# First chunk of a fused attention and two-FFN kernel: a weight piece's head and low part one tick behind its sign, and every second piece's join and low part on VectorE

## The chip, the cores and the metric

One core of a Trainium2 chip runs the whole program. The metric is device microseconds of one execution. TensorE (PE in the profile) multiplies, VectorE (DVE), ScalarE (ACT) and GpSimd (POOL) do the element-wise work, and SyncE (SP) issues the transfers. Each engine takes its instructions in the order in which they were written, and waits for others by semaphores.

## The reference, cut to what matters

```python
x = attention(q, k, v)             # 4 batches, 8 heads, 576 x 64; half the heads local, half strided
h = x @ w_in                       # 2304 x 512 @ 512 x 2048
x = (h - np.tanh(h)) @ w_out       # 2048 x 512
g, val = x @ w_gate, x @ w_val     # 512 x 1536 each
return (g / (1 + np.exp(-g)) * val) @ w_out2
```

Everything is float32 (the host reads pairs of float32 weights as int64). The change touches how `w_in` and `w_out` are made ready, and one small step of the attention's softmax.

## The kernel before, in words

The 2304 tokens are worked through in five chunks of 512 (one of 256). For each chunk the first FFN runs over 16 column blocks, f = 0 to 15: twelve matmuls of 128x512 give `ps_h` (`first_part`), `bend` takes tanh on ScalarE (L520) and subtracts on VectorE (L521), `parts` splits the result into a high and a low half on ScalarE (L527) and VectorE (L528), and twelve matmuls add the block to `ps_acc` (`second`, one iteration later). Every product is taken as three matmuls, high by low, high by high and low by high (L191 to L193), so every weight must exist as a high half and a low half.

During the first chunk two more streams share the engines. One is the attention of the second batch, in twelve groups: its scores (PE, L265), mask and row maximum (VectorE, three times L273), exp (ScalarE, L282), the reciprocal of the row sum (ScalarE L290 adds 1e-9, VectorE L294), the multiplication by it (GpSimd, L296), transposes (PE, L308), the copy of them (VectorE, L312) and the product with v (PE, L320). The other is the feed: the weights arrive as 32 pieces of 128x512 int64 words, each of them read as a low int32 word and a high one, and every piece goes through

- `high` and `low` on ScalarE (L124, L127),
- `rebase` on VectorE: `clamp` (L130) and `shift` (L134),
- `join` on GpSimd: an int32 addition (L142),
- `sign` on VectorE (L146),
- `head` on ScalarE, which rounds to the high half (L152), and `rest` on GpSimd, which subtracts it for the low half (L155).

Pieces 0 to 3 (`PRE`) are made during the attention of the first batch. From then on `Feed.tick` is called twice in an iteration: once after `bend` and the product with v, and once after `second` and exp. Tick t starts the load of piece t + 2, takes piece t through `high` and `low`, piece t - 1 through `rebase` and `join`, and piece t - 2 through `sign`, `head` and `rest`. Iteration f multiplies with pieces 2f - 1 and 2f, and its ticks are 4 + 2f and 5 + 2f. The order on each engine is the order in which the code is written; no scheduler moves it in this part of the program.

Of the kernel before, what the change touches and what calls it, by code (L numbers as in the profile page):

```python
# [7 lines left out]
F32 = mybir.dt.float32  # L8
# [5 lines left out]
AF = mybir.ActivationFunctionType  # L14
ALU = mybir.AluOpType
# [18 lines left out]
BV = 2  # L34
# [21 lines left out]
STREAMED = (3, 7, 11, 15)  # L56
# [5 lines left out]
PRE = 4  # L62
# [11 lines left out]
def model_kernel(ctx: ExitStack, tc: tile.TileContext, q, k, v, mask, ident, sq, sk, sv, smask, w1, w2, out):  # L74
    nc = tc.nc
# [34 lines left out]
        return mpool.tile([P, 512], F32, tag=mtags[-1], name="m")  # L110

    class Piece:
        def __init__(self, key, src, place, then=None):
            self.key, self.src, self.place, self.then = key, src, place, then

        def load(self):
            self.st = stage.tile([P, 512], I64, tag="st", name="st")
# [21 lines left out]

        def join(self):  # L140
            mi = self.m.bitcast(I32)
            nc.gpsimd.tensor_tensor(out=mi, in0=mi, in1=self.lo, op=ALU.add)  # L142

        def sign(self):
            mi = self.m.bitcast(I32)
# [6 lines left out]
            nc.scalar.copy(self.w[:, 0, :], self.m)  # L152

        def rest(self):
            nc.gpsimd.tensor_tensor(out=self.w[:, 1, :], in0=self.m, in1=self.w[:, 0, :].bitcast(F32), op=ALU.subtract)  # L155
            if self.then:
                self.then(self.w)

    class Feed:
# [18 lines left out]
        def tick(self):  # L178
            t = self.at
            self.at += 1  # L180
            self.load(t + 3)
            self.do(t, "high", "low")
            if t - 1 >= self.since:
                self.do(t - 1, "rebase", "join")
            if t - 2 >= self.since:
                self.do(t - 2, "sign", "head", "rest")

    def mm3(ps, w, c0, xh, xl, start, stop, goes_on=False):

# [5 lines left out]
    with tc.manual_schedule():  # L195
# [56 lines left out]
        class Group:  # L252
# [25 lines left out]
            def exp(self):  # L278
                w = self.w
                self.sm = att.tile([P, 16], F32, tag="sm", name="sm", bufs=3)[:, :GB]  # L280
                for i in range(GB):
                    nc.scalar.activation(  # L282
                        self.s[:, i, :w], self.s[:, i, :w], AF.Exp, scale=-1.0, bias=self.mx[:, i:i + 1],
                        **({"accum_out": self.sm[:, i:i + 1]} if self.b else {}),
                    )

            def norm(self, eng):
                w = self.w
                if self.b:
                    nc.scalar.activation(self.sm, self.sm, AF.Copy, bias=1e-9)  # L290
                else:
                    nc.vector.tensor_reduce(out=self.sm, in_=self.s[:, :, :w], axis=AX, op=ALU.add)
                    nc.vector.tensor_scalar(self.sm, self.sm, 1e-9, None, ALU.add)
                nc.vector.reciprocal(self.sm, self.sm)  # L294
                if eng is nc.gpsimd:
                    nc.gpsimd.tensor_tensor(  # L296
                        out=self.s[:, :, :w], in0=self.s[:, :, :w], in1=self.sm.unsqueeze(2).to_broadcast([P, GB, w]),
                        op=ALU.mult,
                    )
                    return  # L300
                for i in range(GB):
                    s, r = self.s[:, i, :w], self.sm[:, i:i + 1]
                    nc.scalar.mul(s, s, r)
# [142 lines left out]
        w1_t, w2_t = {}, {}  # L446
        resident = [f for f in range(NF1) if f not in STREAMED]
        uses = sorted((f + part, part, f) for f in range(NF1) for part in range(2))
# [3 lines left out]
        def slot_of(f, part, c=0):  # L452
            if f in STREAMED:
                return 2 * NRES + (c * NS + stream.index((f, part))) % NSS
            return 2 * resident.index(f) + part

        def piece1(f, part):
            def spill(w):
                nc.sync.dma_start(out=w1s[stream.index((f, part))], in_=w.bitcast(F32))

            return Piece((f, part), w1[f, :, part * 512:(part + 1) * 512], lambda: wtile(f"w{slot_of(f, part)}"),
                         spill if f in STREAMED else None)

        def wtile(tag):
            return wpool.tile([P, 2, 512], F32R, tag=tag, name=tag)
# [13 lines left out]
        def restore():  # L479
            while fetching:  # L480
                c, i = fetching.pop(0)
                w = w1_t[stream[i]] = wtile(f"w{slot_of(*stream[i], c)}")
                nc.sync.dma_start(out=w.bitcast(F32), in_=w1s[i])

        feed1 = Feed([piece1(f, part) for _, part, f in uses], w1_t)

        def halves(xh, xl, src, dh, dl):
            nc.scalar.copy(dh, src)
# [29 lines left out]
        def bend(ps, n):  # L518
            t = epool.tile([P, CHUNK], F32, tag="e", name="t")
            nc.scalar.activation(t[:, :n], ps[:, :n], AF.Tanh)  # L520
            nc.vector.tensor_tensor(out=ps[:, :n], in0=ps[:, :n], in1=t[:, :n], op=ALU.subtract)  # L521
            return ps
# [54 lines left out]
        ahead, late, order = [], [], PAIRS  # L577
# [168 lines left out]
        class Quad:  # L746
# [54 lines left out]
            def prepare(self):  # L801
# [23 lines left out]
                for s in range(2):  # L825
# [27 lines left out]
                    s4 = flow.add("G", 0.78, lambda pool=pool: pool("d", right, "b", right, "m", right, ALU.subtract, "bm"), (s2, s3))  # L853
                    h1 = flow.add("A", 0.4, half, (a, *((h1,) if s else ())), None if s else slots)
                    self.ends[s, 4] = flow.add("V", 0.45, rest, (h1,))
                    later.append((s2, s4))
                for i, (name, src, products) in enumerate((("w2", "m", (5, 6)), ("w3", "d", (7, 3)))):
# [157 lines left out]
        for c, (c0, n) in enumerate(CHUNKS1):  # L1015
# [10 lines left out]
            for f in range(NF1):  # L1026
# [26 lines left out]
                t = bend(ps, n)  # L1053
# [91 lines left out]
        late = ctx.enter_context(tc.tile_pool(name="late", bufs=1, side="right", reuse_waits="tile"))  # L1145
# [158 lines left out]
        for t in range(2):  # L1304
# [18 lines left out]
            for p in ORDER3:  # L1323
                flow.until(lambda: len(G[t, p]) == NQ and all(left(p, q)[0] is not None for q in range(NQ)),
                           [*W3[{1: 0, 2: 1, 4: 1, 5: 2, 6: 2}.get(p, 3)], *G3[t, p]])
                for m in range(2):
                    place = {1: "a", 6: "a", 5: "a", 3: "a", 2: "b", 7: "c", 4: "c"}[p]
# [131 lines left out]
```

## Time and profile before

| | us |
|---|---|
| median of 3 runs (lowest, highest) | 923.49 (920.88, 923.81) |
| the profiled execution | 920.19 |
| its span | 918.3 |
| PE busy in the span | 880.8 (96%) |
| VectorE, ScalarE, GpSimd busy | 644.5, 458.7, 337.5 |
| first chunk, from the tanh of f = 2 to that of f = 12 | 78.91 (58.30 to 137.21) |
| from there to the second chunk's first tanh | 30.53 |

PE's busy time is nearly the span, so the kernel is bound by PE wherever PE finds its inputs ready. The page's picture in 40 slices of 23 us shows PE at 8 tenths in the first three slices and in the seventh and eighth (138 to 184 us), and at 9 in nearly all others. TensorE's granted clock is at full level (2.4 GHz) from the third slice on. To read how an iteration of the first chunk goes, one takes the engines' rows of one iteration in order of time and sees which row begins late, and which lasts longer than others of its kind. A row's duration includes the time for which the instruction was held up after it had begun.

### The profile page before, as it was taken

The page shows a single profiled execution, that of the slowest core. Times are in us where ns is not written, and L with a number is a line of the kernel's source. Part 1 is how long each engine was busy: PE and PEld are TensorE (multiplying, and loading weights), DVE is VectorE, ACT ScalarE, POOL GpSimd, SP SyncE. Part 2 cuts the span into 40 slices and gives each one's busy share as a digit, 9 for nine tenths or more (in the row PEclk, how much of TensorE's full clock was granted, in tenths as well). Part 3 has the DMA queues.
Part 4 walks back from the last instruction along what each step waited for, and adds up shares of the span by engine and source line. Part 5 has one row for each costly group of instructions (what it writes and reads, how often), then busy time and mean ns, then how long its engine had stood idle before and what let it go on. Part 6 is the DMA issues. An engine that isn't in the chain of part 4 may idle for free. (4 is left out here: it accounts for less than half of the span.)

```text
span 918.3 us, 14160 instructions
## 1 busy us (share of the span) xinstructions
PE 880.8 (96%) x4918; PEld 722.3 (79%) x4918; DVE 644.5 (70%) x1222; ACT 458.7 (50%) x1034; POOL 337.5 (37%) x284
## 2 busy tenths in 40 slices
PE   8889998899999999999999988999999999999998
PEld 6567776777877778998887776888888887888888
DVE  6778786677776787326886785788877777966451
ACT  5577775534244523225555454555545446655431
POOL 2578887385526553001503421535544320000000
PEclk9899999999999999999999999999999999999999
DMA  8464743632343210426636642535452568968551
GB/s 272 154 195 155 255 158 113 241 110 82 103 140 118 69 46 24 146 85 237 221 92 205 207 149 82 183 117 165 154 184 87 200 216 291 344 229 278 198 202 42
DMA packets 66215, 150.38 MB, mean 164 GB/s; under 512 B 7200, under 2 KB 13344, under 8 KB 66144
## 3 DMA queue, kind: packets, MB, share of 16 engines
q1 hardware_dynamic: 65568, 149.04, 48.3%
q8 instruction: 39, 0.64, 0.3%
q10 hardware_dynamic: 576, 0.43, 0.2%
q14 instruction: 32, 0.26, 0.1%
HBM read 105.93 MB, written 43.52 MB: 163 GB/s over the span
## 5 line engine op out<-in xcount | busy, mean ns | idle before, releaser
L193 PE MATMUL ps_acc<-sl 128*128 128x512 f32 (+1 forms) x336 | 126.7, 377 | 5.0 <-DVE sl L738 5.0
L191 PE MATMUL ps_acc<-sl 128*128 128x512 f32 (+1 forms) x336 | 126.8, 377 | 3.4 <-ACT t L1206 3.4
L191 PE MATMUL ps_acc<-gl,w 128*128 128x512 f32 (+1 forms) x320 | 123.2, 385 | 3.4 <-DVE gl L528 3.3
L192 PE MATMUL ps_acc<-sl 128*128 128x512 f32 (+1 forms) x336 | 126.4, 376 | 0.0
L191 PE MATMUL ps_h<-xl,w 128*128 128x512 f32 (+1 forms) x320 | 121.1, 379 | 1.9 <-DVE gl L528 1.9
L193 PE MATMUL ps_h<-xh,w 128*128 128x512 f32 (+1 forms) x320 | 118.5, 370 | 0.7 <-POOL w L155 0.7
L193 PE MATMUL ps_acc<-gh,w 128*128 128x512 f32 (+1 forms) x320 | 118.5, 370 | 0.0
L192 PE MATMUL ps_acc<-gh,w 128*128 128x512 f32 (+1 forms) x320 | 118.3, 370 | 0.0
L192 PE MATMUL ps_h<-xh,w 128*128 128x512 f32 (+1 forms) x320 | 118.1, 369 | 0.0
L142 POOL TENSOR_TENSOR sl<-sl,st 128x512 int32<-128x512 int32 x36 | 52.0, 1450 | 164.6 <-DVE sl L134 134.2
L520 ACT ACTIVATE t<-ps_h 128x512 f32<-128x512 f32 (+1 forms) x80 | 44.0, 550 | 110.9 <-PE ps_h L193 110.9
L521 DVE TENSOR_TENSOR ps_h<-ps_h,t 128x512 f32<-128x512 f32 (+1 forms) x80 | 51.5, 643 | 65.5 <-ACT t L520 65.1
L976 DVE TENSOR_TENSOR sl<-sl 128x512 fp32r<-128x512 f32 (+1 forms) x120 | 73.9, 669 | 28.5 <-ACT sl L972 27.8
L528 DVE TENSOR_TENSOR gl<-ps_h,gh 128x512 fp32r<-128x512 f32 (+1 forms) x80 | 51.1, 638 | 39.5 <-ACT gh L527 38.0
L972 ACT CAST sl<-sl 128x512 fp32r<-128x512 f32 (+1 forms) x120 | 65.7, 599 | 25.2 <-DMA sl<-gd 19.0
L193 PEld LDWEIGHTS ps_acc<-sl 128*128 128x128 f32 x336 | 63.7, 190 | 17.2 <-DVE sl L738 5.9
L191 PEld LDWEIGHTS ps_acc<-sl 128*128 128x128 f32 x336 | 63.7, 190 | 16.8 <-ACT t L1206 5.5
L191 PEld LDWEIGHTS ps_acc<-gl,w 128*128 128x128 f32 x320 | 60.3, 188 | 18.5 <-DVE gl L528 6.0
L386 POOL TENSOR_TENSOR pr<-skv,sq 128x576 f32<-128x576 f32 (+8 forms) x40 | 56.3, 1437 | 50.2 <-DVE sc L393 30.6
L191 PE MATMUL ps_a<-sl 128*128 128x512 f32 (+1 forms) x192 | 70.3, 366 | 2.7 <-DVE t L1167 2.7
L192 PEld LDWEIGHTS ps_acc<-sl 128*128 128x128 f32 x336 | 63.6, 189 | 11.2
L193 PEld LDWEIGHTS ps_h<-xh,w 128*128 128x128 f32 x320 | 60.5, 189 | 11.8 <-POOL w L155 1.5
(125 smaller groups left out, 1960.9 us busy)
## 6 DMA issues: line engine op xcount, KB each, us to landing
st<-in_w SPq DMA_DIRECT2D x68, 512.0 KB, 4.7
gd<-t SPq DMA_DIRECT2D x84, 256.0 KB, 2.1
sl<-gd SPq DMA_DIRECT2D x84, 256.0 KB, 4.5
w<-w1s SPq DMA_DIRECT2D x32, 512.0 KB, 3.5
w3s<-sl SPq DMA_DIRECT2D x24, 256.0 KB, 4.0
sl<-w3s SPq DMA_DIRECT2D x24, 256.0 KB, 5.4
x2d<-o SPq DMA_DIRECT2D x18, 256.0 KB, 3.2
out_t<-t SPq DMA_DIRECT2D x18, 256.0 KB, 2.1
```

Source lines behind the costliest of these rows:

```text
L142: nc.gpsimd.tensor_tensor(out=mi, in0=mi, in1=self.lo, op=ALU.add)
L191: nc.tensor.matmul(ps, lhsT=wh, rhs=xl, start=start, stop=False, skip_group_check=goes_on)
L192: nc.tensor.matmul(ps, lhsT=wh, rhs=xh, start=False, stop=False, skip_group_check=goes_on)
L193: nc.tensor.matmul(ps, lhsT=wl, rhs=xh, start=False, stop=stop, skip_group_check=goes_on)
L386: nc.gpsimd.tensor_tensor(out=t, in0=x, in1=y, op=ALU.mult)
L520: nc.scalar.activation(t[:, :n], ps[:, :n], AF.Tanh)
L521: nc.vector.tensor_tensor(out=ps[:, :n], in0=ps[:, :n], in1=t[:, :n], op=ALU.subtract)
L528: nc.vector.tensor_tensor(out=gl[:, :n], in0=t[:, :n], in1=gh[:, :n].bitcast(F32), op=ALU.subtract)
L972: nc.scalar.copy(got[0][:, 0, :n], got[0][:, 1, :n].bitcast(F32))
L976: nc.vector.tensor_tensor(out=w[:, 1, :n], in0=w[:, 1, :n].bitcast(F32), in1=w[:, 0, :n].bitcast(F32), op=ALU.subtract)
```

## The change

Three things change.

1. In `tick`, piece t - 3 now gets `head` (it was t - 2, together with its sign). `rest` of that piece follows at once in odd ticks, and stands at the end of the tick in even ones. `sign` of piece t - 2 comes before `high`, `low`, `rebase` and `join` of the later pieces.
2. Pieces from 4 on with an odd number get `join` and `rest` on VectorE; the others stay on GpSimd. That is fourteen pieces, 5 to 31.
3. In the second batch's attention the addition of 1e-9 stands directly behind exp, and no longer at the start of the next iteration.

```diff
         def join(self):
             mi = self.m.bitcast(I32)
-            nc.gpsimd.tensor_tensor(out=mi, in0=mi, in1=self.lo, op=ALU.add)
+            self.eng.tensor_tensor(out=mi, in0=mi, in1=self.lo, op=ALU.add)
...
         def rest(self):
-            nc.gpsimd.tensor_tensor(out=self.w[:, 1, :], in0=self.m, in1=self.w[:, 0, :].bitcast(F32), op=ALU.subtract)
+            self.eng.tensor_tensor(out=self.w[:, 1, :], in0=self.m, in1=self.w[:, 0, :].bitcast(F32), op=ALU.subtract)
...
             self.load(t + 3)
-            self.do(t, "high", "low")
-            if t - 1 >= self.since:
-                self.do(t - 1, "rebase", "join")
-            if t - 2 >= self.since:
-                self.do(t - 2, "sign", "head", "rest")
+            late = t % 2 == 0
+            for back, *steps in (
+                (3, "head", *(() if late else ("rest",))), (2, "sign"), (0, "high", "low"), (1, "rebase", "join"),
+                (3, *(("rest",) if late else ())),
+            ):
+                if t - back >= self.since:
+                    self.do(t - back, *steps)
...
+                if 0 < self.b < BV:
+                    nc.scalar.activation(self.sm, self.sm, AF.Copy, bias=1e-9)
...
-                if self.b:
+                if self.b >= BV:
                     nc.scalar.activation(self.sm, self.sm, AF.Copy, bias=1e-9)
-                else:
+                if not self.b:
...
-        def piece1(f, part):
+        def piece1(i, f, part):
...
-                         spill if f in STREAMED else None)
+                         spill if f in STREAMED else None, nc.vector if i >= PRE and i % 2 else nc.gpsimd)
```

VectorE's order in the middle of the first chunk, before, from the copy of one group's transposes (L312) to the last feed step ahead of the next group's mask and maximum; `m` is the piece being made, `ps_h` and `gl` belong to the FFN:

```order
L312 COPY pt<-ps_a 80x384
L528 TENSOR_TENSOR gl<-ps_h,gh 128x512
L130 TENSOR_SCALAR m<-m 128x512
L134 TENSOR_SCALAR m<-m 128x512
L146 SCALAR_TENSOR_TENSOR m<-st,m 128x512
L294 RECIPROCAL sm<-sm 128x3
L521 TENSOR_TENSOR ps_h<-ps_h,t 128x512
L130 TENSOR_SCALAR m<-m 128x512
L134 TENSOR_SCALAR m<-m 128x512
L146 SCALAR_TENSOR_TENSOR m<-st,m 128x512
```

The same stretch now (lines are up to four higher: L316 is L312, L532 is L528, L298 is L294, L525 is L521):

```order
L316 COPY pt<-ps_a 80x384
L532 TENSOR_TENSOR gl<-ps_h,gh 128x512
L146 SCALAR_TENSOR_TENSOR m<-st,m 128x512
L130 TENSOR_SCALAR m<-m 128x512
L134 TENSOR_SCALAR m<-m 128x512
L298 RECIPROCAL sm<-sm 128x3
L525 TENSOR_TENSOR ps_h<-ps_h,t 128x512
L146 SCALAR_TENSOR_TENSOR m<-st,m 128x512
L130 TENSOR_SCALAR m<-m 128x512
L134 TENSOR_SCALAR m<-m 128x512
L142 ISA m<-st,m 128x1024
L155 TENSOR_TENSOR w_1220<-m,w_1220 128x512
```

The two signs (L146) have moved ahead of the clamp and shift of their tick, and the odd pieces' join and rest stand at the end. The join has become a custom instruction on 1024 halves of words (`ISA`), since VectorE takes 512 int32 words so.

GpSimd's order over two iterations, before; `s` is a group's softmax, `w` a finished weight:

```order
L155 TENSOR_TENSOR w_1007<-m,w_1007 128x512
L296 TENSOR_TENSOR s<-s,sm 128x3x80
L142 TENSOR_TENSOR m<-m,st 128x512
L155 TENSOR_TENSOR w_1046<-m,w_1046 128x512
L142 TENSOR_TENSOR m<-m,st 128x512
L155 TENSOR_TENSOR w_1096<-m,w_1096 128x512
L296 TENSOR_TENSOR s<-s,sm 128x3x80
L142 TENSOR_TENSOR m<-m,st 128x512
L155 TENSOR_TENSOR w_1135<-m,w_1135 128x512
L142 TENSOR_TENSOR m<-m,st 128x512
```

And now (L300 is L296):

```order
L155 TENSOR_TENSOR w_1087<-m,w_1087 128x512
L142 TENSOR_TENSOR m<-m,st 128x512
L300 TENSOR_TENSOR s<-s,sm 128x3x80
L155 TENSOR_TENSOR w_1176<-m,w_1176 128x512
L142 TENSOR_TENSOR m<-m,st 128x512
L300 TENSOR_TENSOR s<-s,sm 128x3x80
L155 TENSOR_TENSOR w_1272<-m,w_1272 128x512
L142 TENSOR_TENSOR m<-m,st 128x512
L300 TENSOR_TENSOR s<-s,sm 128x288
```

An iteration had two joins, two rests and a multiplication on GpSimd, and has one of each now; the join stands directly ahead of the multiplication, and the rest ahead of the join.

## Rows read from the trace of the kernel before

**Rows 1.** Busy time by engine, two stretches: us, then each engine's.

```profile
core 0: us, PE busy (x) PEld busy (x) DVE busy (x) ACT busy (x) POOL busy (x), PEclk, DMA share, GB/s
58.30:137.21 78.91, 72.71 (x498) 54.73 (x497) 64.56 (x161) 58.44 (x161) 65.67 (x51) 1.00 0.60 194
137.21:167.74 30.53, 26.63 (x131) 19.71 (x130) 21.11 (x35) 17.44 (x37) 18.60 (x15) 1.00 0.34 120
```

**Rows 2.** Waits from 50 to 165 us: in total, times, longest.

```profile
ACT w L152 <- DVE m L146: 29.9, 26, 2.4
...
PE ps_a L308 <- POOL s L296: 7.4, 11, 1.5
```

**Rows 3.** VectorE in order of time, one iteration: start us, us.

```profile
84.47 0.68 DVE L146 SCALAR_TENSOR_TENSOR m<-st,m 128x512 int32<-128x512 int32 x1
85.07 0.23 DVE L273 CUSTOM_DVE_ANT_0 s<-ps_a,mask_s 128x80 f32<-128x80 f32 x1
...
85.55 0.54 DVE L312 COPY pt<-ps_a 80x384 f32<-80x384 f32 x1
86.32 0.69 DVE L528 TENSOR_TENSOR gl<-ps_h,gh 128x512 fp32r<-128x512 f32 x1 [0.22 <-ACT gh L527]
86.93 0.94 DVE L130 TENSOR_SCALAR m<-m 128x512 f32<-128x512 f32 x1
87.90 0.43 DVE L134 TENSOR_SCALAR m<-m 128x512 int32<-128x512 int32 x1
...
90.21 0.70 DVE L521 TENSOR_TENSOR ps_h<-ps_h,t 128x512 f32<-128x512 f32 x1 [0.31 <-ACT t L520]
90.81 0.82 DVE L130 TENSOR_SCALAR m<-m 128x512 f32<-128x512 f32 x1
```

**Rows 4.** GpSimd in order of time, the same iteration.

```profile
86.28 1.30 POOL L155 TENSOR_TENSOR w<-m,w 128x512 fp32r<-128x512 f32 x1
88.46 1.63 POOL L142 TENSOR_TENSOR m<-m,st 128x512 int32<-128x512 int32 x1 [0.88 <-POOL w L155]
90.05 1.31 POOL L155 TENSOR_TENSOR w<-m,w 128x512 fp32r<-128x512 f32 x1
91.31 0.77 POOL L296 TENSOR_TENSOR s<-s,sm 128x240 f32<-128x240 f32 x1
```

**Rows 5.** VectorE's clamp and shift with GpSimd idle, around 50 us.

```profile
49.66 0.42 DVE L130 TENSOR_SCALAR m<-m 128x512 f32<-128x512 f32 x1
...
50.11 0.43 DVE L134 TENSOR_SCALAR m<-m 128x512 int32<-128x512 int32 x1
```

**Rows 6.** GpSimd's join and multiplication around 51 us.

```profile
50.67 1.31 POOL L142 TENSOR_TENSOR m<-m,st 128x512 int32<-128x512 int32 x1 [2.39 <-ACT s L282]
51.94 0.59 POOL L296 TENSOR_TENSOR s<-s,sm 128x240 f32<-128x240 f32 x1
```

**Rows 7.** Lines L738 and L890 in the whole run: ns minimum, median, maximum.

```profile
L738 DVE TENSOR_TENSOR sl<-sl x67: 677/684/1800, 426.4 to 734.3; 128x512 fp32r<-128x512 f32 x67
L890 DVE TENSOR_TENSOR sl<-sl x8: 1211/1219/2225, 458.1 to 540.0; 128x1024 f32<-128x1024 f32 x8
```

**Rows 8.** ScalarE in order of time: first exp, high, head of an iteration.

```profile
86.18 0.36 ACT L282 ACTIVATE s<-s,mx 128x80 f32<-128x80 f32 x1
...
87.23 0.67 ACT L124 ACTIVATE m<-st 128x512 f32<-128x512 f32 x1
...
88.96 0.62 ACT L152 CAST w<-m 128x512 fp32r<-128x512 f32 x1 [0.48 <-DVE m L146]
```

**Rows 9.** ScalarE's tanh of f = 2, of f = 12, of the second chunk's f = 0.

```profile
58.30 0.58 ACT L520 ACTIVATE t<-ps_h 128x512 f32<-128x512 f32 x1
...
137.21 0.58 ACT L520 ACTIVATE t<-ps_h 128x512 f32<-128x512 f32 x1
...
167.74 0.60 ACT L520 ACTIVATE t<-ps_h 128x512 f32<-128x512 f32 x1 [2.08 <-PE ps_h L193]
```

More of the change, by code (lines that the diff above doesn't have):

```diff
@@ L112, in model_kernel, with __init__ @@
     class Piece:
-        def __init__(self, key, src, place, then=None):
-            self.key, self.src, self.place, self.then = key, src, place, then
+        def __init__(self, key, src, place, then=None, eng=nc.gpsimd):
+            self.key, self.src, self.place, self.then, self.eng = key, src, place, then, eng
         def load(self):
@@ L483, in restore @@
                 nc.sync.dma_start(out=w.bitcast(F32), in_=w1s[i])
-        feed1 = Feed([piece1(f, part) for _, part, f in uses], w1_t)
+        feed1 = Feed([piece1(i, f, part) for i, (_, part, f) in enumerate(uses)], w1_t)
         def halves(xh, xl, src, dh, dl):
```

## The prediction

> **What bounds the kernel now.** I read the busy time by stretches first. From the tanh of f = 2 to that of f = 12 of the first chunk, ten full iterations, PE is busy for 72.71 of 78.91 us [rows 1, 9]: an iteration takes 7.89 us, and PE idles for 0.62 of it. In the rest of the chunk it is busy for 26.63 of 30.53 us [rows 1]. So at most 6.2 + 3.9 = 10.1 us are to be had where the change works, and later chunks gain or lose only by starting earlier or later.
>
> Then the waits. PE waits 11 times, 7.4 us in all, for GpSimd's softmax multiplication before a transpose, and ScalarE spends 29.9 us with its head waiting for VectorE's sign [rows 2]. Both are what the change goes at.
>
> Third, the two timelines side by side, for who makes GpSimd late. The reader is to compare rows of one kind. VectorE's clamp takes 0.42 us and its shift 0.43 when GpSimd is idle [rows 5]. In the iteration the clamp at 86.93 takes 0.94, and ends at 87.87: 0.42 behind 87.45, while GpSimd's rest ends at 87.58 [rows 3, 4]. The clamp at 90.81 takes 0.82 and ends 0.42 behind 91.21, with GpSimd's rest ending at 91.36. Both were held until about 0.13 to 0.15 us before the end of GpSimd's record. The other way round, GpSimd's join takes 1.31 us undisturbed [rows 6] but 1.63 at 88.46 [rows 4], when it starts while a sign runs. So VectorE's clamp, shift and sign and all of GpSimd's instructions hold each other off; one at a time gets through, and the one that waits comes next. Instructions of VectorE that read PSUM are not held: the mask (0.23) and L521 (0.70) have their usual lengths beside GpSimd's work [rows 3]. The stage is therefore bound by this alternation between VectorE and GpSimd, with 65.67 us of GpSimd and 64.56 of VectorE in 78.91 [rows 1], and PE's waits are its result.
>
> **The change part by part.** It takes from GpSimd, in an iteration, one join and one rest: 1.31 + 1.30 = 2.61 us [rows 4, 6]. That leaves under 4 of its 6.6 us, so GpSimd is no longer short of time. It gives VectorE these two.
>
> The rest on VectorE is a float32 subtraction of two SBUF operands, 128x512: 0.684 us median [rows 7]. The join is not in the trace. It handles 512 words, as 1024 halves. By the sign, which reads the same strided words, it would be 0.68 [rows 3]; by L890 with its 1024 elements, 1.22 [rows 7]. I take 0.78, since the bytes are the sign's, and keep 0.68 and 1.22 for the range. Below 0.68 there is nothing: no two-operand row of 512 words is shorter. The Trainium skill, VectorE: DVE Perf Modes, "What auto-detection actually checks", has two-source instructions on 16-bit operands of step 1 run at double rate; by that the 1024 halves would take no longer than 512 words, and the sum would be about 1 us lower. No row here shows such an instruction.
>
> Head behind its sign by a tick: the 29.9 us of ScalarE's waiting go, since a sign is a tick old when its head comes. That frees tanh, which stood behind the head, and I count 0.5 us for it in the first two iterations. ScalarE is not the bound afterwards. The 1e-9 addition, moved behind exp, is done before the reciprocal comes to its turn; the reciprocal is hidden below, so I count nothing for it.
>
> What is late next is VectorE. I lay one iteration of it out in the new order, from the end of an even piece's shift to the next such end. Back-to-back instructions start about 0.08 us before the record of the one ahead ends (85.07 against 84.47 + 0.68) [rows 3], so the pitches below are shorter than durations.
> - GpSimd's join starts 0.13 behind the shift (88.33 to 88.46) [rows 3, 4] and takes 1.31 [rows 6]. The next sign needs just this join: 1.44. The reciprocal and L521 (0.70) are hidden in it.
> - GpSimd's multiplication stands right behind the join and gets in ahead of the sign: 0.59 less 0.13 for the 80-wide groups, more for the 96-wide: 0.50 [rows 6].
> - Sign 0.60 (84.47 to 85.07), clamp 0.45, shift 0.43 [rows 3, 5].
> - Join 0.70 and rest 0.60, as pitches.
> - Mask and maximum 0.48 (85.07 to 85.55), copy 0.46, L528 0.61 (86.32 to 86.93), sign 0.60, clamp 0.45 [rows 3, 5].
> - Shift 0.43, held by GpSimd's rest. This rest comes when ScalarE has done three exps (86.18 to 87.23, 1.05 us) and a head (0.62) [rows 8], begun with the mask: some 1.8 to 2.1 us behind it, which is just when clamp and shift are due (0.48 + 0.46 + 0.61 + 0.60 = 2.15). Of its 1.30 less 0.13 I count 0.95 as VectorE's loss; between 0 and 1.17 is possible.
>
> The sum is 1.44 + 0.50 + 1.48 + 1.30 + 2.60 + 1.38 = 8.70 us, against 7.89: 0.81 more. PE (7.27 busy) and ScalarE (5.84) [rows 1] lie beside it. Ten iterations lose 8.1 us. The rest of the chunk comes to 8.2 for an iteration without the mask and three of 8.70 - 0.50 - 0.48 - 0.46 = 7.3 without any softmax, 30.1 against 30.5: about even. With 0.5 us won at the start, that is 7.6 to 8.1; I take 8.
>
> A weight comes a tick later now. It is still made in the iteration before the one that uses it, some 8 us ahead, so I cost that at nothing; with VectorE behind by more than an iteration it would appear as PE waiting for a rest. The loads come from a five-buffer pool whose buffers are freed by signs, which come earlier in the tick; nothing there. The loss is carried to the end, for the later chunks are ordered behind the first on PE.
>
> By the profiled execution, 920.19 + 8 = 928.2; that run is 3.3 under the median of those shown, so against the median 923.5 + 8 = 931.5.
>
> **The rivals.**
>
> *GpSimd's relief wins.* If the two stalls of VectorE, 0.50 and 0.95, don't arise, because the rest falls beside the copy and L528, which read PSUM, and the multiplication behind the sign, an iteration is 8.70 - 1.45 = 7.25, and PE's 7.27 decides. Then all of PE's idle time goes: 923.5 - 10.1 = 913.4. For it speaks that GpSimd has half its time free. Against it: the rest cannot start before exp and head, which wait for the mask, and these put it on the clamp, not on the copy. The Trainium skill, GPSIMD Engine Reference, "4.1 Engine selection", puts element-wise additions on VectorE, as about twice as fast there. That is true of each instruction here (0.68 against 1.30 for a rest), and by it alone this rival would be the forecast.
>
> *One stall stays.* With the rest hidden and the multiplication not, or the other way round, an iteration is 7.75 to 8.2: between -1.4 and +3 us, around 923.
>
> *The join at 1.22.* As the forecast, with 0.44 more in each of some thirteen iterations: +5.7, so 937.
>
> *The change does not do what it says:* if VectorE still waited for GpSimd's pieces, its sign would; it does, for the even ones, and that is in the sum.
>
> **How the numbers follow.** The forecast 0.57, the slow join 0.15, one stall 0.14, relief 0.14. The two slower cases lie above 926.3 but for a tail of 0.02. Of the middle case 0.06 is faster by over 0.3% (under 920.7), 0.05 within, 0.03 slower; 0.3%, 2.8 us, is about what can be told from no change. So faster 0.20, same 0.07, slower 0.73. The forecast's own range is 927 to 935. Eight tenths need most of the slow join and the middle case: 919 to 938.
>
> **What would show it.** In the changed profile tanh starts of neighbouring iterations would be 8.5 to 8.9 us apart. VectorE would be busy for more than 90% of the ten iterations and GpSimd for some 40%. The odd ticks' clamp or shift would last 1.2 us or more beside a rest of GpSimd's, and the sign of an even piece would wait for GpSimd's join or last longer than 1 us. ScalarE's head would no longer wait for a sign. It is wrong if iterations are 7.9 us or less, if shift and clamp keep their 0.43, or if the join takes less than 0.6 or over 1.3.

## The result, and the profile after

The changed kernel takes 933.42 us (median of 4 runs, 931.52 to 934.88), the kernel before 922.74 in the runs beside it (4 runs, 920.88 to 923.81): a ratio of 1.0117, 95% interval 1.0091 to 1.0143. Slower, as forecast, 1.9 us above the forecast and inside its own range.

Busy time by stretches in the profile after, in the columns of [rows 1]: the ten iterations, then the rest of the first chunk.

```profile
61.81:147.87 86.06, 74.00 (x505) 55.08 (x500) 77.07 (x180) 58.12 (x161) 33.59 (x31) 1.00 0.59 178
147.87:180.21 32.34, 27.97 (x136) 20.95 (x137) 25.85 (x43) 18.21 (x38) 9.62 (x9) 1.00 0.32 112
```

An iteration takes 8.61 us (7.89 before), and the rest of the chunk 1.81 us more than 30.53. VectorE is busy for 77.07 of 86.06 us (90%), and GpSimd's share has fallen from 83% to 39%. The profiled execution takes 934.88 us, 14.7 more than before. Of these, 3.95 arise ahead of the first tanh (50.78 against 46.83), where nothing was changed; a second profile of the same kernel (below) has it at 48.25, so they are not put down to the change. 8.5 arise from there to the second chunk's first tanh, and 2.2 behind that. These last are not put down to the change either: 2.8 are lost between 570 and 600 us, where the granted clock is 0.89 in this execution and 1.00 in the same stretch, counted from the second chunk's first tanh, of the second profile and of the kernel before; the remainder of the run wins some of it back.

VectorE in order of time, one iteration after, against [rows 3]. L525 was L521, L298 L294, L275 L273, L316 L312 and L532 L528; the number in brackets is the engine's idle time just before the row, and what ended it. The dots behind the first shift stand for the reciprocal (0.16 us).

```profile
86.03 0.42 DVE L130 TENSOR_SCALAR m<-m 128x512 f32<-128x512 f32 x1
86.48 1.40 DVE L134 TENSOR_SCALAR m<-m 128x512 int32<-128x512 int32 x1
...
87.88 0.67 DVE L525 TENSOR_TENSOR ps_h<-ps_h,t 128x512 f32<-128x512 f32 x1
89.36 1.06 DVE L146 SCALAR_TENSOR_TENSOR m<-st,m 128x512 int32<-128x512 int32 x1 [0.81 <-POOL m L142]
90.34 0.41 DVE L130 TENSOR_SCALAR m<-m 128x512 f32<-128x512 f32 x1
90.79 0.43 DVE L134 TENSOR_SCALAR m<-m 128x512 int32<-128x512 int32 x1
91.25 0.69 DVE L142 CUSTOM_DVE_ANT_0 m<-st,m 128x1024 uint16<-128x1024 uint16 x1
91.86 0.68 DVE L155 TENSOR_TENSOR w<-m,w 128x512 fp32r<-128x512 f32 x1
92.46 0.23 DVE L275 CUSTOM_DVE_ANT_0 s<-ps_a,mask_s 128x80 f32<-128x80 f32 x1
...
92.94 0.55 DVE L316 COPY pt<-ps_a 80x384 f32<-80x384 f32 x1
93.42 0.68 DVE L532 TENSOR_TENSOR gl<-ps_h,gh 128x512 fp32r<-128x512 f32 x1
94.01 0.68 DVE L146 SCALAR_TENSOR_TENSOR m<-st,m 128x512 int32<-128x512 int32 x1
94.61 0.42 DVE L130 TENSOR_SCALAR m<-m 128x512 f32<-128x512 f32 x1
95.06 1.39 DVE L134 TENSOR_SCALAR m<-m 128x512 int32<-128x512 int32 x1
```

GpSimd beside it, against [rows 4, 6]:

```profile
86.13 1.46 POOL L155 TENSOR_TENSOR w<-m,w 128x512 fp32r<-128x512 f32 x1 [4.84 <-DVE m L146]
88.01 1.32 POOL L142 TENSOR_TENSOR m<-m,st 128x512 int32<-128x512 int32 x1 [0.42 <-DVE sm L298]
89.28 0.59 POOL L300 TENSOR_TENSOR s<-s,sm 128x240 f32<-128x240 f32 x1
```

Read the two together. The shift at 86.48 ends at 87.88, 0.43 behind 87.45; GpSimd's rest ends at 87.59. So the shift was held until 0.14 before the end of that record. GpSimd's join begins 0.13 behind the shift's end, and the sign at 89.36 begins 0.03 behind the join's end. That sign then lasts 1.06 instead of 0.68: GpSimd's multiplication, in order right behind the join, got in ahead of it. These are the two stalls that the forecast named, and the 0.81 is VectorE's only idle time in the iteration.

The waits of the same stretch (50 to 175 us), against [rows 2]:

```profile
POOL w L155 <- DVE m L146: 48.7, 10, 4.9
...
PE ps_h L195 <- DVE w L155: 16.4, 13, 2.7
DVE m L146 <- POOL m L142: 9.3, 11, 1.1
...
ACT w L152 <- DVE m L146: 2.7, 2, 2.2
```

ScalarE's head waits for 2.7 us in all (29.9 before). GpSimd now waits for VectorE, and PE for the rest that VectorE makes, not for the softmax.

### The profile page after: what moved, and what is told of

It reads as the page before. It is cut to its first block, busy times and chain, and to the rows that moved or that the text cites. A ratio compares the mean times of both kernels' runs of the same rounds, so it can differ in the third digit from the quotient of the medians.

```text
span 933.0 us, 14169 instructions
## 1 busy us (share of the span) xinstructions
PE 887.5 (95%) x4918; PEld 727.0 (78%) x4918; DVE 661.5 (71%) x1250; ACT 459.8 (49%) x1034; POOL 293.7 (31%) x256
## 5 line engine op out<-in xcount | busy, mean ns | idle before, releaser
L195 PE MATMUL ps_h<-xh,w 128*128 128x512 f32 (+1 forms) x320 | 120.8, 378 | 16.4 <-DVE w L155 16.4
L194 PE MATMUL ps_h<-xh,w 128*128 128x512 f32 (+1 forms) x320 | 119.6, 374 | 0.0
L525 DVE TENSOR_TENSOR ps_h<-ps_h,t 128x512 f32<-128x512 f32 (+1 forms) x80 | 51.2, 640 | 65.7 <-ACT t L524 65.3
L532 DVE TENSOR_TENSOR gl<-ps_h,gh 128x512 fp32r<-128x512 f32 (+1 forms) x80 | 50.9, 636 | 32.5 <-ACT gh L531 31.0
```

The source lines that it names most:

```text
L194: nc.tensor.matmul(ps, lhsT=wh, rhs=xh, start=False, stop=False, skip_group_check=goes_on)
L195: nc.tensor.matmul(ps, lhsT=wl, rhs=xh, start=False, stop=stop, skip_group_check=goes_on)
L532: nc.vector.tensor_tensor(out=gl[:, :n], in0=t[:, :n], in1=gh[:, :n].bitcast(F32), op=ALU.subtract)
```

## The experiments

Two explanations stand against each other. The first is the forecast's: the new order puts GpSimd's join right ahead of a sign that needs it, its multiplication ahead of that sign too, and its rest on a clamp or shift. The second: VectorE has more work, two instructions more in an iteration, wherever they stand. Each kernel was profiled and timed beside the kernel before. Diffs are against the changed kernel.

**The order alone.** The new order, every join and rest on GpSimd.

```diff
-                         spill if f in STREAMED else None, nc.vector if i >= PRE and i % 2 else nc.gpsimd)
+                         spill if f in STREAMED else None, nc.gpsimd)
```

> The new order of the ticks alone; every join and rest stays on GpSimd. Theory A (the order): a sign now stands directly behind its GpSimd join, so VectorE waits out the join in both ticks, and GpSimd's rest still holds a clamp or shift; iterations of 8.5 to 8.8 us and a time of 929 to 935 us, as slow as the whole change without VectorE doing any more work. Theory B (the added work): what costs is the join and rest that VectorE took on, 1.37 us an iteration; without them an iteration is 7.9 us or less, and the time 915 to 924 us.

Measured: 934.17 us, ratio 1.0129 (1.0105 to 1.0153). With VectorE relieved of all that the change gave it, the loss is as large. The iteration takes 8.79 on average, or 8.53 without the first one, which takes 11.13 (PE waits there for a rest of GpSimd's, 3.1 us). It is another iteration, though: VectorE waits for a tanh, and its clamp is held by two rests of GpSimd's that follow each other. VectorE, then GpSimd:

```profile
85.01 1.51 DVE L130 TENSOR_SCALAR m<-m 128x512 f32<-128x512 f32 x1
...
87.83 0.70 DVE L525 TENSOR_TENSOR ps_h<-ps_h,t 128x512 f32<-128x512 f32 x1 [0.75 <-ACT t L524]
```

```profile
83.27 2.97 POOL L155 TENSOR_TENSOR w<-m,w 128x512 fp32r<-128x512 f32 x2
```

So the order by itself is enough for the loss, but this run does not show that it is by the same two stalls.

**The move alone.** The old order, odd pieces on VectorE.

```diff
-            late = t % 2 == 0
-            for back, *steps in (
-                (3, "head", *(() if late else ("rest",))), (2, "sign"), (0, "high", "low"), (1, "rebase", "join"),
-                (3, *(("rest",) if late else ())),
...
+            self.do(t, "high", "low")
+            if t - 1 >= self.since:
+                self.do(t - 1, "rebase", "join")
+            if t - 2 >= self.since:
+                self.do(t - 2, "sign", "head", "rest")
```

> The old order of the ticks; the odd pieces' join and rest on VectorE. Theory A (the order): a whole tick lies between a join and its sign, so VectorE waits for no join; its added work replaces time in which GpSimd held it; iterations of 7.9 to 8.2 us, a time of 921 to 927 us. Theory B (the added work): VectorE's 1.37 us more per iteration come on top, iterations of 8.5 us or more, 930 us or more.

Measured: 925.43 us, ratio 1.0034 (1.0016 to 1.0052), 8.08 an iteration. The move costs about 3 us in the old order and nothing measurable in the new one (933.42 with it, 934.17 without). The trace shows a new wait and a hold: the rest now stands on VectorE in the tick of its sign and head, and waits for the head there. How much of the 3 us they carry was not tried.

```profile
85.46 1.00 DVE L155 TENSOR_TENSOR w<-m,w 128x512 fp32r<-128x512 f32 x1 [0.73 <-ACT w L152]
```

**GpSimd's rest made small.** The even pieces' rest on 16 columns; the remaining columns of their low half are filled by ScalarE with other data, so those weights are not the reference's.

```diff
-            self.eng.tensor_tensor(out=self.w[:, 1, :], ...
+            n = 16 if self.small else 512
+            self.eng.tensor_tensor(out=self.w[:, 1, :n], ...
...
```

> The changed kernel with the even pieces' rest on GpSimd cut to 16 of 512 columns (the rest of the low half is filled with other numbers by ScalarE, in its idle time ahead of exp, so the output is not the reference's). Theory A, as in the prediction's sum: the shift loses its hold of 0.95 us and nothing else is near, so iterations fall from 8.61 to about 7.7 us and the time by 9 to 11 us, to 922 to 925. Theory A2: tanh is next, since in the changed kernel it ends only 0.2 us ahead of VectorE's L525; iterations stay at 8.3 to 8.5 us and the time falls by 2 to 3 us.

Measured: 918.28 us, ratio 0.995 (0.9931 to 0.9968), 7.67 an iteration. That is 0.94 less than 8.61, and the shift's row shows where it went (L532 is here the subtraction behind tanh, L525 above):

```profile
89.98 0.43 DVE L134 TENSOR_SCALAR m<-m 128x512 int32<-128x512 int32 x1
...
91.21 0.70 DVE L532 TENSOR_TENSOR ps_h<-ps_h,t 128x512 f32<-128x512 f32 x1 [0.72 <-ACT t L531]
```

1.40 less 0.43 is 0.97. One hold of one instruction so carries the whole of the loss and some more. It also shows VectorE's chain as the pace: what was taken from it came out of the iteration nearly one to one. Theory A2 priced tanh as the next limit. VectorE does wait for tanh now, 0.72 us, but in the time in which it would wait for GpSimd's join anyway, so this costs nothing. The time is under theory A's 922 to 925; the rest of the chunk, which it left out, is 3.0 us shorter too (29.30 against 32.34).

**The multiplication made small.** GpSimd's multiplication of the first chunk on 4 columns of each group; the other softmax weights stay unnormalised.

```diff
+                    w = 4 if self.b == 1 else w
                     nc.gpsimd.tensor_tensor(
```

> The changed kernel with GpSimd's softmax multiplication of the first chunk's groups cut to 4 columns (the rest of the weights stays unnormalised, so part of the computation is left out). In the changed kernel's trace the multiplication takes 0.59 us, starts right behind GpSimd's join and ahead of VectorE's sign, and the sign then takes 1.06 instead of 0.69 us. If VectorE's chain sets the pace, the sign comes back to about 0.69 and an iteration falls from 8.61 by 0.37 to 0.5 us, to 8.1 to 8.25; ten to twelve such iterations give 4 to 6 us: 927.5 to 930. Rival: PE or ScalarE sets the pace and VectorE's holds lie beside it, then 8.6 an iteration and 932 to 934.

Measured: 926.26 us, ratio 1.0038 (1.0014 to 1.0061), 8.20 an iteration, 0.41 less. VectorE's sign is back at its length, and still waits for the join:

```profile
86.91 0.69 DVE L146 SCALAR_TENSOR_TENSOR m<-st,m 128x512 int32<-128x512 int32 x1 [0.81 <-POOL m L142]
```

1.06 less 0.69 is 0.37, so this stall too is paid in full. The iteration is as expected; the time is 1.2 us under the range.

**The sign behind the rebase and join of the tick.** The wait for the join should go, since a clamp and a shift stand between.

```diff
-                (3, "head", ...), (2, "sign"), (0, "high", "low"), (1, "rebase", "join"),
+                (3, "head", ...), (0, "high", "low"), (1, "rebase", "join"), (2, "sign"),
```

> The changed kernel with one step moved: in a tick, the sign of piece t - 2 comes behind rebase and join of piece t - 1 instead of ahead of them. Theory A (the order): the sign of an even piece no longer stands right behind its join, so VectorE's idle 0.8 us in each iteration goes, less what the clamp then loses to the same join; iterations of 8.0 to 8.3 us, 925 to 930 us. Theory B (the added work): VectorE has as much to do as before and is as slow, iterations of 8.5 us or more, 932 to 934 us.

Measured: 923.00 us, ratio 1.0011 (0.9993 to 1.0030), 8.20 an iteration. The wait is gone, and 0.41 us of the iteration with it, but the hold has moved: GpSimd's rest now catches the other sign, its join the clamp.

```profile
84.57 0.87 DVE L130 TENSOR_SCALAR m<-m 128x512 f32<-128x512 f32 x1
...
90.35 1.78 DVE L146 SCALAR_TENSOR_TENSOR m<-st,m 128x512 int32<-128x512 int32 x1
```

GpSimd's rest there runs from 90.26 for 1.31 us. With a sign so placed the kernel is neither slower nor faster, by more than can be told, than before the change. The iteration is theory A's; the time is 2 us under its range; the rest of the chunk is shorter too (29.65 against 32.34).

**The addition of 1e-9 back at its old place.**

```diff
-                if 0 < self.b < BV:
-                    nc.scalar.activation(self.sm, self.sm, AF.Copy, bias=1e-9)
...
-                if self.b >= BV:
+                if self.b:
```

> The changed kernel with the addition of 1e-9 put back to the front of the normalisation, as before the change (ScalarE does it there, later than behind the exps). I counted this part of the change at nothing, since VectorE's reciprocal lies in its wait for GpSimd's join (0.81 us of idle time before the even piece's sign). If so: 932 to 935, 8.6 to 8.7 an iteration. Rival: the reciprocal and so the multiplication come later, out of the place between join and sign, and the multiplication then holds another instruction or none: 8.2 an iteration and about 929, or over 8.9 and 937.

Measured: 931.59 us, ratio 1.0091 (1.0056 to 1.0126), 8.66 an iteration. No difference from the changed kernel that can be told, as counted; the time is 0.4 us under the range expected.

**The other half of the pieces on VectorE.** The same instructions as in the changed kernel; the even pieces go to VectorE, and the ticks' parity is exchanged.

```diff
-            late = t % 2 == 0
+            late = t % 2 == 1
...
-                         spill if f in STREAMED else None, nc.vector if i >= PRE and i % 2 else nc.gpsimd)
+                         spill if f in STREAMED else None, nc.vector if i >= PRE and i % 2 == 0 else nc.gpsimd)
```

> The changed kernel with the other half of the pieces on VectorE: the even pieces have join and rest there, the odd ones on GpSimd, and the tick in which the rest comes late is exchanged too. All instructions and their number are those of the changed kernel; only where GpSimd's work falls in the two-tick iteration is another. If the loss is that GpSimd's join ends just ahead of its sign and its rest falls on the clamp and shift that follow, then here the join of the odd piece is followed by VectorE work that does not wait for it (mask, copy, L532), and an iteration takes 7.5 to 8.0 us: 914 to 923. Rival: the loss is VectorE's added work or the later weights, which are the same here: 8.5 to 8.7 an iteration, 931 to 935.

Measured: 919.21 us, ratio 0.9958 (0.9933 to 0.9983), 7.68 an iteration. This is the plainest evidence against the second explanation: VectorE has just as much to do, and the kernel is 11 to 14 us faster than with the odd pieces (930.45 and 933.42). GpSimd's join now starts beside the mask, and VectorE has the rest of the mask, the copy and L532 to do until the sign, which neither waits nor is held. The rest still holds a clamp. VectorE, then GpSimd:

```profile
86.26 1.51 DVE L130 TENSOR_SCALAR m<-m 128x512 f32<-128x512 f32 x1
...
89.71 0.69 DVE L146 SCALAR_TENSOR_TENSOR m<-st,m 128x512 int32<-128x512 int32 x1
```

```profile
85.75 1.74 POOL L155 TENSOR_TENSOR w<-m,w 128x512 fp32r<-128x512 f32 x1
88.37 1.31 POOL L142 TENSOR_TENSOR m<-m,st 128x512 int32<-128x512 int32 x1 [0.88 <-POOL w L155]
```

**An order for each tick.** Even pieces on VectorE, the sign always with a tick's other work between it and its join.

```diff
...
+                ((3, "head"), (1, "rebase"), (3, "rest"), (0, "high", "low"), (2, "sign"), (1, "join"))
+                if t % 2 else
+                ((1, "rebase"), (3, "head"), (2, "sign"), (3, "rest"), (0, "high", "low"), (1, "join"))
...
```

> Even pieces on VectorE as in the run before, and an order of its own for each of two ticks: odd tick head, rebase of the newest, rest, high and low, sign, join; even tick rebase, head, sign, rest, high and low, join. A sign so stands a tick's work away from its join, and GpSimd's rest starts beside VectorE's instructions that read PSUM. The same instructions in number and size as in the changed kernel. If placement is the whole of it, an iteration is bounded by PE's 7.27 us busy: 7.25 to 7.5, and 911 to 917, faster than both kernels. Rival: moving half the joins and rests to VectorE costs as much as the alternation gives back: 7.9, about 922.

Measured: 914.75 us, ratio 0.9908 (0.9877 to 0.9939), faster than both kernels. An iteration takes 7.40, and the rest of the chunk 27.36:

```profile
60.50:134.45 73.95, 73.41 (x499) 54.70 (x499) 73.26 (x182) 58.21 (x160) 37.27 (x30) 1.00 0.66 208
134.45:161.81 27.36, 27.15 (x134) 20.69 (x135) 24.84 (x42) 18.23 (x38) 11.21 (x9) 1.00 0.38 132
```

PE (73.41) and VectorE (73.26) are both busy all through the 73.95 us. VectorE's rows of an iteration show that one hold has even stayed, on the shift, but no wait; what this hold still costs was not tried:

```profile
84.78 1.40 DVE L134 TENSOR_SCALAR m<-m 128x512 int32<-128x512 int32 x1
...
89.64 0.69 DVE L146 SCALAR_TENSOR_TENSOR m<-st,m 128x512 int32<-128x512 int32 x1
```

Which of the two engines sets 7.40 was not tried.

**That order with everything on GpSimd.** The run before, with all pieces' join and rest on GpSimd.

> The order of the mixed run (914.75 us, 7.40 an iteration), with all joins and rests back on GpSimd. It completes the square of order and engine: old and new order have been run with and without the move. The order as the whole cause of the gain: 914 to 918. GpSimd's time as the bound again: it had 65.7 of 78.9 us busy before the change, four instructions of 1.3 to 1.6 and a multiplication of 0.6 in an iteration, nearly every one of them held by or holding VectorE; then 7.8 to 8.3 an iteration and 920 to 928.

Measured: 919.88 us, ratio 0.998 (0.996 to 1.0001), no difference from the kernel before that can be told; 7.95 an iteration. That is the time expected with GpSimd as the bound, at its lower edge, but not quite for that reason: in the ten iterations GpSimd is busy for 69.19 of 79.47 us, and VectorE, with its holds, for 78.18. Both signs of an iteration are held:

```profile
84.57 1.76 DVE L146 SCALAR_TENSOR_TENSOR m<-st,m 128x512 int32<-128x512 int32 x1
...
88.59 1.77 DVE L146 SCALAR_TENSOR_TENSOR m<-st,m 128x512 int32<-128x512 int32 x1
```

So the good order needs the move: 5 to 7 us of its gain come with it (5.1 by the medians, 0.7% by the ratios to the kernel before).

**The changed kernel once more.**

> The changed kernel once more, unedited, for the start of its profiled execution: its first tanh stood at 50.78 us there against 46.83 before, with a late query load and a lower granted clock ahead of it. If that is of the one execution: first tanh at 48 to 50.5 here, iterations 8.61 again, time 931 to 935. If it is the change's: 50.8 again.

Measured: 930.45 us, ratio 1.0094 (1.0057 to 1.0132). First tanh at 48.25, 8.60 an iteration, 33.21 for the rest of the chunk. So the late start was of the one execution; the time is 0.5 us under the range expected.

The rest of the chunk is 0.9 us longer than in the first profile, all of it in the step of f = 12 (10.17 against 9.22). In both profiles PE first idles there for 2.68 us, waiting for the rest that VectorE makes. In the first the granted clock stays at 1.00 after that. Here it falls to 0.50, which is 1.2 GHz, in the two microseconds from 154 (the columns of [rows 1]), and a matmul takes 0.63 us instead of 0.39. Tanh begins 3.64 us behind the rest's end, against 2.66 in the first profile:

```profile
154.00:156.00 2.00, 2.00 (x16) 1.25 (x14) 0.30 (x1) 0.52 (x1) 1.29 (x1) 0.50 0.01 4
```

```profile
154.39 0.63 PE L194 MATMUL ps_h<-xh,w 128*128 128x512 f32 x1
```

The runs with the small multiplication and with the addition back have such a step too (9.88 and 10.41), with a granted clock of 0.50 and 0.53 behind PE's wait. Since the first profile has the wait without the lower clock, the wait alone does not decide it.

All together, in us:

| order of the tick | all on GpSimd | half on VectorE |
|---|---|---|
| as before | 922 to 923 | 925.43 (odd) |
| as changed | 934.17 | 933.42 and 930.45 (odd); with the parity exchanged, 919.21 (even) |
| one for each tick | 919.88 | 914.75 (even) |

## Why the prediction was right, point by point

*The sum of the iteration: right, and term by term.* From the end of one shift at 87.88 to the next at 96.45 (95.06 + 1.39) the rows give 8.57; the forecast said 8.70.

| step | said | measured |
|---|---|---|
| GpSimd's join, until the sign | 1.44 | 1.48 (87.88 to 89.36) |
| multiplication ahead of the sign | 0.50 | 0.38 (89.36 to 90.34, less the sign's 0.60) |
| sign, clamp, shift | 1.48 | 1.51 |
| join and rest on VectorE | 1.30 | 1.21 (91.25 to 92.46) |
| mask to clamp | 2.60 | 2.60 (92.46 to 95.06) |
| shift, held by GpSimd's rest | 1.38 | 1.39 |

The runs with the small rest and the small multiplication confirm both stalls by taking them away: 0.94 and 0.41 of an iteration, against 0.95 and 0.50 said.

*The join on VectorE:* 0.69, not 0.78, and far from the 1.22 of the slow rival. The Trainium skill, VectorE: DVE Perf Modes, "What auto-detection actually checks", led to about this number, by a double rate for 16-bit operands; that the 1024 halves take no longer than 512 words agrees with it. One operand here is every second word of a 64-bit tile, which is not the step of 1 that the page asks for, and no run here shows why the instruction is still that short.

*The start:* f = 0 to f = 2 takes 11.03 us in both profiles of the changed kernel and 11.47 before: 0.44 won, 0.5 said. ScalarE's head stopped waiting, as said.

*The rest of the chunk: the step that failed.* "About even" was 30.1 us; the two profiles have 32.34 and 33.21. The forecast took four iterations of VectorE's pace, 8.2 and three of 7.3. ScalarE's tanh rows after, from f = 12 to the second chunk:

```profile
147.87 0.58 ACT L524 ACTIVATE t<-ps_h 128x512 f32<-128x512 f32 x1
157.09 0.60 ACT L524 ACTIVATE t<-ps_h 128x512 f32<-128x512 f32 x1 [1.39 <-PE ps_h L195]
163.88 0.60 ACT L524 ACTIVATE t<-ps_h 128x512 f32<-128x512 f32 x1 [1.42 <-PE ps_h L195]
171.69 0.60 ACT L524 ACTIVATE t<-ps_h 128x512 f32<-128x512 f32 x1 [5.17 <-PE ps_h L195]
180.21 0.60 ACT L524 ACTIVATE t<-ps_h 128x512 f32<-128x512 f32 x1 [2.09 <-PE ps_h L195]
```

The last step, 8.52, was costed at 7.3: but no piece is joined or signed there any more, so VectorE's pace does not apply, and it took as long before, from this row to the second chunk's first tanh [rows 9], 8.49:

```profile
159.25 0.59 ACT L520 ACTIVATE t<-ps_h 128x512 f32<-128x512 f32 x1
```

That is 1.2 of the 2.2 us missed in the first profile. The other 1.0 lies in the three steps ahead, 23.82 against 22.8. There GpSimd's rest, without a mask to wait for, comes earlier, and falls on VectorE's own join in the iterations of f = 12 and f = 14. VectorE, then GpSimd:

```profile
152.12 1.71 DVE L142 CUSTOM_DVE_ANT_0 m<-st,m 128x1024 uint16<-128x1024 uint16 x1
153.75 0.68 DVE L155 TENSOR_TENSOR w<-m,w 128x512 fp32r<-128x512 f32 x1
...
166.69 1.74 DVE L142 CUSTOM_DVE_ANT_0 m<-st,m 128x1024 uint16<-128x1024 uint16 x1
168.35 0.68 DVE L155 TENSOR_TENSOR w<-m,w 128x512 fp32r<-128x512 f32 x1
```

```profile
152.02 1.26 POOL L155 TENSOR_TENSOR w<-m,w 128x512 fp32r<-128x512 f32 x1 [1.28 <-ACT w L152]
...
166.59 1.29 POOL L155 TENSOR_TENSOR w<-m,w 128x512 fp32r<-128x512 f32 x1 [1.46 <-ACT w L152]
```

The joins take 1.02 and 1.05 over their 0.69, the odd rest behind them comes later by as much, and PE waits for it: tanh begins 2.66 us behind the rest's end in both (154.43 to 157.09, 169.03 to 171.69). So the lateness of a weight, costed at nothing, is the path here: the forecast laid PE beside VectorE's chain, and in these two iterations PE's work follows it. The 0.9 more of the second profile stands beside the lower clock after that same wait of PE's, which no term of the forecast had. As a sum, ten iterations cost 7.15 instead of 8.1, and the rest of the chunk 1.8 to 2.7 instead of nothing: two errors of opposite sign, and that they so nearly cancel is luck. 7.15 - 0.44 + 1.8 to 2.7 is 8.5 to 9.4; the medians moved by 10.7 and 8.6. Where the rest of the 10.7 lies is open; one execution of that median, the profiled one, lost 2.2 us behind the first chunk.

*"A weight comes a tick later, at nothing": right in the ten iterations, but not for the reason given.* I had the odd weight ready some 8 us ahead. In fact PE waits for it in each of the ten, 12.1 us in all, which is all of PE's idle time there (86.06 less 74.00). This costs nothing because there is slack behind it. PE, then ScalarE, in the iteration above:

```profile
92.60 0.50 PE L195 MATMUL ps_h<-xh,w 128*128 128x512 f32 x1 [1.22 <-DVE w L155]
...
94.78 0.39 PE L195 MATMUL ps_h<-xh,w 128*128 128x512 f32 x1
```

```profile
95.12 0.67 ACT L127 ACTIVATE st<-st 128x512 int32<-128x512 uint32 x1
95.69 0.57 ACT L524 ACTIVATE t<-ps_h 128x512 f32<-128x512 f32 x1
```

VectorE's rest ends at 92.54, PE goes on at once, and `ps_h` is complete at 95.17. Tanh begins 0.52 later, directly behind ScalarE's own work; it ends at 96.26, and VectorE takes its result at 96.46. That subtraction could come later still, by the 0.8 us that VectorE then waits for the join, as the run with the small rest shows. In the rest of the chunk this slack is gone.

*GpSimd's relief wins:* wrong for the changed kernel, but nearly its time can be had. It was 913.4; with the pieces and the order exchanged 914.75 was measured, with the same instructions, though one hold stayed there. The Trainium skill, GPSIMD Engine Reference, "4.1 Engine selection", is borne out for single instructions (0.69 and 0.68 on VectorE, 1.32 and 1.30 to 1.46 on GpSimd), and the measured times say what follows from it alone: moving half the joins and rests gives +0.3%, nothing that can be told, or -0.7%, by the order in which they stand. *One stall stays* is what the small multiplication, the small rest and the exchanged parity measured: 8.20, 7.67 and 7.68 an iteration against 7.75 to 8.2 said.

## What to carry to other kernels

Where two engines hold each other off, lay one period of the in-order queue out from the trace, with each hold and each wait as a term: here that gave 8.70 for 8.57. Ask of every moved step not only how long it takes, but what the other engine then does beside it, in the stretches without the usual neighbours too. And before a move is given up as too slow, exchange its parity or its place: the same instructions in the same number made 930.5 to 933.4, 919.2 and 914.8 us. A wait that one engine's delay gives another has to be followed to where its slack ends: here PE's wait cost nothing in one stretch, and in the next it was the path, in some executions with a lower clock behind it.

## What the hardware showed beyond that

A hold ends a little before the holder's record: 0.14 us before the end of GpSimd's rest for the shift (87.45, that is 87.88 less 0.43, against 87.59) and for the sign behind the multiplication (89.73, that is 90.42 less 0.69, against 89.87). VectorE's 16-bit form of the join, which no row showed before, is held like the rest: 1.71 and 1.74 instead of 0.69. The Trainium skill, SBUF — State Buffer, "SBUF: two separate sides", tells of VectorE and GpSimd sharing a pair of ports that one instruction at a time has for its whole length; the holds here are of that kind, with those 0.14 us as the difference.
